# One store for 1/z, keys loaded ahead of queries, and new weights of a list scheduler in an attention and gated-convolution kernel

## The chip, the cores and the metric

The kernel runs on one core of a Trainium2 chip. The metric is the device time of one execution in microseconds (us); lower is better. TensorE is called PE below, VectorE DVE, ScalarE ACT, GpSimd POOL, and SyncE, which issues every DMA of this kernel, SP.

## The reference

```python
def _attn_ref(q, kv, w_sr):            # q: 4 x 12288 x 128, kv: 4 x 384 x 32 x 128
    kv_pool = kv.reshape(B, H // r, r, W // r, r, C).mean(axis=(2, 4))   # r = 4
    kv_flat = kv_pool.reshape(B, -1, C) @ w_sr                           # 768 keys of 128
    k = v = kv_flat
    s = scale * (q @ k.transpose(0, 2, 1))
    s = s - s.max(-1, keepdims=True)
    a = np.exp(s)
    a /= a.sum(-1, keepdims=True) + 1e-09
    return a @ v

def _moe_ref(x, w_val, conv_w, w_out):  # x is the attention's result
    ...
    for k in range(K):                  # 5 taps along the sequence
        gate_pre += conv_w[k][None, None, :] * xp[:, k:k + S, :]
    gate = 1.0 / (1.0 + np.exp(-gate_pre))
    val = x @ w_val
    return (gate * val @ w_out).astype(np.float32)
```

## The kernel before

**Tiling.** There are 4 batches, each with 12288 queries and 768 keys of 128 numbers. A group is 512 queries of one batch, 24 groups to a batch, 96 in all, numbered 0 to 95. Within a group a score tile `s` holds 128 queries (on partitions) by 768 keys; there are four, j = 0 to 3. The host hands over q and kv with the 128 channels on partitions; the kernel writes its result with channels on partitions too.

**A batch's set-up** (`setup`): kv comes in 16 pieces (`kvt`, line 257, six buffers), DVE sums each piece over its 16 pooled positions (L266), PE projects the sums with w_sr (L287), and ACT and DVE split the keys into two parts `kh`, `kl` and the values into `vh`, `vl`. From the second batch on the loads and sums are spread over the groups of the batch before it, about one piece to a group.

**A group** (`group`): q is loaded for two groups at once (L419); ACT and POOL split it into `qh`, `ql`. Per score tile PE does six matmuls (L445), DVE takes the row maximum (L457), ACT the exponential with its row sum z (L471). For j = 0 to 2 ACT and DVE then split the exponentials into two f16 parts `hl` (L487, L498) and SP has them transposed by DMA into `pt` (L510, one DMA for j = 0 and 1, one for j = 2). For j = 3 PE transposes the f32 exponentials in six blocks (L532), and ACT and DVE write the split straight into `pt` (L545, L549). Then 18 matmuls (L610) sum values times `pt` into one PSUM bank `av`.

**1/z** has to lie along the free axis of all partitions to multiply `av`, whose partitions are channels. POOL adds 1e-9 (L569), DVE takes the reciprocal of a 128 x 4 tile (L573) and transposes it in 32 x 32 blocks (L577). Row j of each 32-row block then holds 32 queries of tile j. Four DMAs of 4 rows each write these to a DRAM scratch `rd` (L583), and one DMA reads it back broadcast to all partitions, `rb` (L589). DVE multiplies, x = av * down * rb (L628).

**After x**: POOL makes four of the five taps (L677) and adds them up (L686), ACT makes one tap (L666) and the tanh (L701); PE does x @ w_val (L705), DVE the product (L709), PE the output matmul (L714), ACT the move out of PSUM (L719), and SP stores two groups at once (L739).

**What is single.** There is one `av` bank, so the first L610 matmul of a group has to wait until L628 of the group before has read `av`; one `m` bank for L705 and L714; and three `s` tiles, which the score tiles and the PE transposes share.

**What sets the order.** Every instruction is a step with an engine, an estimated duration, a due time and what it waits for, takes and frees. `Plan.order` is a list scheduler in the program itself: again and again it places, on the engine that can begin first, the step with the least due time among those that could start by then, in times that it estimates. Each engine then carries out its steps strictly in that order. Due times are multiples of `PERIOD` (a group's planned length) and `AV_DUE` written into each step. For SP it reckons 0.06 us per DMA issue, and a DMA queue that takes the steps' durations one after the other:

```python
            if e == "SP":
                free[e] = t + 0.06
                dma = max(dma, t + self.DMA_LEAD) + s.dur
                s.end = dma + self.DMA_TAIL
```

## Time and profile before

| | |
|---|---|
| median of 3 runs | 1136.8 us (1133.98 to 1137.78) |
| the profiled execution's own time | 1133.29 us |
| its span, first to last instruction | 1131.5 us |
| busy share of PE, DVE, ACT, POOL | 93%, 81%, 77%, 78% |
| the 16 DMA engines: share of SP's queue | 86.4% |
| the same execution's granted PE clock, mean | 0.992 of full speed |

The busy shares count an instruction from its start to its end; matmuls overlap one another, so PE's share says that it is seldom without work, not that it is at its peak. The span is cut into four parts further below: the load of the first keys up to about 31 us, a ramp up to the first x at 62.7 us, 95 steps from x to x up to 1116.3 us, and 15 us in which the last group's end runs out.

### The profile page before, as it was taken

The page shows a single profiled execution, that of the slowest core. Times are in us where ns is not written, and L with a number is a line of the kernel's source. Part 1 is how long each engine was busy: PE and PEld are TensorE (multiplying, and loading weights), DVE is VectorE, ACT ScalarE, POOL GpSimd, SP SyncE. Part 2 cuts the span into 40 slices and gives each one's busy share as a digit, 9 for nine tenths or more (in the row PEclk, how much of TensorE's full clock was granted, in tenths as well). Part 3 has the DMA queues.
Part 4 walks back from the last instruction along what each step waited for, and adds up shares of the span by engine and source line. Part 5 has one row for each costly group of instructions (what it writes and reads, how often), then busy time and mean ns, then how long its engine had stood idle before and what let it go on. Part 6 is the DMA issues. An engine that isn't in the chain of part 4 may idle for free.

```text
span 1131.5 us, 16498 instructions
## 1 busy us (share of the span) xinstructions
PE 1050.6 (93%) x5056; PEld 667.7 (59%) x5056; DVE 918.4 (81%) x1280; ACT 869.8 (77%) x1559; POOL 884.2 (78%) x1049
## 2 busy tenths in 40 slices
PE   0799999999999999999999899999999999999996
PEld 0565656666656656666666555665666666666662
DVE  6788887878888988878888888887887788787784
ACT  1577877888777878878888777888888888887872
POOL 1167887888978788888878778888888888888872
PEclk9899999999999999999999999999999999999997
DMA  9488999888899999898999899978888898987774
GB/s 336 101 189 181 224 213 201 164 185 197 200 214 205 230 211 208 186 178 175 215 237 199 188 194 209 202 165 180 190 172 178 188 189 167 178 205 154 154 158 98
DMA packets 488968, 215.54 MB, mean 190 GB/s; under 512 B 455728, under 2 KB 455856, under 8 KB 488880
## 3 DMA queue, kind: packets, MB, share of 16 engines
q1 hardware_dynamic: 488880, 214.49, 86.4%
q8 instruction: 41, 0.67, 0.2%
q14 instruction: 47, 0.39, 0.1%
HBM read 75.83 MB, written 25.36 MB: 89 GB/s over the span
## 4 chain that ended last, share of the span: by engine, by line
PE 68%; DVE 11%; DMA 9%; SPq 4%; issue 3%; ACT 3%; POOL 1%; DVEq 0%
PE s L445 26%; PE av L610 24%; PE m L705 6%; PE m L714 6%; PE s L532 5%; DMA kvt<-in_kv 4%; DMA rb<-rd 3%; DVE nm L457 3%; SPq L510 2%; DVE hl L498 2%; DVE x L628 2%; DVE pool L266 1%; DVE pt L549 1%; SPq L583 1%; ACT s L471 1%
## 5 line engine op out<-in xcount | busy, mean ns | idle before, releaser
L686 POOL TENSOR_TENSOR gate<-gate,tap 128x512 f32<-128x512 f32 x376 | 481.6, 1281 | 14.2
L457 DVE TENSOR_REDUCE nm<-s 128x1 f32<-128x768 f32 x384 | 363.9, 951 | 79.9 <-PE s L445 77.8
L610 PE MATMUL av<-pt,vh 128*128 128x512 f16 x1152 | 374.6, 381 | 19.1 <-DVE x L628 11.9
L471 ACT ACTIVATE s<-s,nm 128x768 f32<-128x768 f32 x288 | 251.8, 874 | 111.8 <-DVE nm L457 110.6
L498 DVE SCALAR_TENSOR_TENSOR hl<-s,hl 128x768 f16<-128x768 f32 x288 | 271.8, 945 | 13.4 <-ACT hl L487 12.4
L445 PE MATMUL s<-kh,qh 128*128 128x512 f32 (+1 forms) x768 | 258.8, 418 | 19.3 <-DVE hl L498 9.6
L487 ACT ACTIVATE hl<-s 128x768 f16<-128x768 f32 x288 | 232.9, 811 | 3.8
L610 PE MATMUL av<-pt,vl 128*128 128x512 f16 x576 | 218.8, 380 | 0.0
L610 PEld LDWEIGHTS <-vh 128*128 128x128 f16 x1152 | 109.6, 98 | 179.0 <-issue 77.0
L445 PE MATMUL s<-kl,qh 128*128 128x512 f32 (+1 forms) x768 | 198.9, 340 | 0.0
L445 PE MATMUL s<-kh,ql 128*128 128x512 f32 (+1 forms) x768 | 197.6, 338 | 0.0
L677 POOL TENSOR_SCALAR tap<-x,wm 128x512 f32<-128x512 f32 x282 | 191.4, 697 | 0.1
L445 PEld LDWEIGHTS s<-kh,qh 128*128 128x128 f32 x768 | 136.9, 191 | 90.9 <-issue 21.0
L677 POOL TENSOR_SCALAR gate<-x,wm 128x512 f32<-128x512 f32 x94 | 65.4, 696 | 137.7 <-DVE x L628 137.6
L431 POOL TENSOR_TENSOR ql<-q,qh 128x512 fp32r<-128x512 f32 x96 | 122.4, 1275 | 59.8 <-ACT qh L427 59.4
L445 PEld LDWEIGHTS s<-kl,qh 128*128 128x128 f32 x768 | 118.8, 190 | 17.4 <-DVE kl L321 0.5
L445 PEld LDWEIGHTS s<-kh,ql 128*128 128x128 f32 x768 | 118.7, 190 | 17.0
L719 ACT ACTIVATE o<-m 128x512 f32<-128x512 f32 x96 | 57.4, 598 | 67.7 <-PE m L714 67.4
L549 DVE SCALAR_TENSOR_TENSOR pt<-s,pt 128x768 f16<-128x768 f32 x96 | 90.9, 947 | 20.1 <-ACT pt L545 19.8
L714 PE MATMUL m<-h,wm 128*128 128x512 f32 x192 | 100.7, 607 | 3.0 <-DVE h L709 2.0
L705 PE MATMUL m<-x,wm 128*128 128x512 f32 x192 | 99.3, 599 | 3.4 <-DVE x L628 2.7
L532 PE MATMUL s<-ident,p 128*128 128x128 f32 x576 | 96.1, 273 | 1.0 <-ACT p L471 1.0
(59 smaller groups left out, 961.2 us busy)
## 6 DMA issues: line engine op xcount, KB each, us to landing
kvt<-in_kv SPq DMA_DIRECT2D x64, 384.0 KB
q<-in_q SPq DMA_DIRECT2D x48, 512.0 KB
rb<-rd SPq DMA_DIRECT2D x96, 256.0 KB
out<-o SPq DMA_DIRECT2D x47, 512.0 KB
rd<-rt SPq DMA_DIRECT2D x384, 0.5 KB
pt<-hl SPq DMA_TRANSPOSE x192
out<-o SPq DMA_DIRECT2D x2, 256.0 KB
raw<-in_w_moe SPq DMA_DIRECT2D x1, 261.0 KB
```

The source lines that it names most:

```text
L431: nc.gpsimd.tensor_tensor(out=g.ql, in0=g.qt[:, i], in1=g.qh.bitcast(F32), op=ALU.subtract)
L445: nc.tensor.matmul(t[:, c0:c1], a[:, sl], k[:, c0:c1], start=(n == 0), stop=(n == 2))
L457: v.tensor_reduce(out=s.tile, in_=sc.tile[:, :NK], axis=AX.X, op=ALU.max, negate=True)
L471: nc.scalar.activation(out=out, in_=sc.tile[:, :NK], func=AF.Exp, bias=mx.tile, accum_out=g.z[:, j:j + 1])
L487: nc.scalar.activation(out=g.hls[j // 2][:, half, 0], in_=sc.tile[:, :NK], func=AF.Copy, scale=2.0 ** 15)
L498: v.scalar_tensor_tensor(out=hl[:, half, 1], in0=sc.tile[:, :NK], scalar=2.0 ** 15, in1=hl[:, half, 0], op0=ALU.mult, op1=ALU.subtract)
L532: nc.tensor.transpose(state["t"][:, k * P:(k + 1) * P], ex.tile[:, k * P:(k + 1) * P], ident)
L610: nc.tensor.matmul(g.av, st[name][:, k * P:(k + 1) * P], g.pt[:, :, a * NCH + k], start=(n == 0), stop=(n == len(AV) - 1))
L677: nc.gpsimd.tensor_scalar(out=s.tile, in0=src(k), scalar1=w[k], scalar2=1.0, op0=ALU.mult, op1=ALU.mult)
L686: nc.gpsimd.tensor_tensor(out=g.gate, in0=g.gate, in1=tap.tile, op=ALU.add)
L705: nc.tensor.matmul(g.m, wval, g.x[:, HALO:], start=True, stop=True)
L714: nc.tensor.matmul(g.m2, wout, g.h, start=True, stop=True)
```

## The change

- **1/z by one store.** The reciprocal is written to columns 0, 8, 16 and 24 of the 32-wide tile, so that after the block transposition the 16 rows wanted lie at partitions 0, 8, 16, ... 120, and one DMA of 16 rows by 32 writes them. The scratch is then in the order (block of 32 rows, tile j, query). So that this is the output's order too, the host permutes the queries within each 512, and the 18 value matmuls read `pt` in that order: 16 runs of 32 elements instead of 4 runs of 128.
- **Keys first.** The first three loads of q may start in the planner's time only at 9, 24 and 28 us (`FIRST_Q`), the load of the gate's weights (`raw`) at 17 us.
- **Copies drawn together.** Of two DMA steps that could start, a copy that follows a copy gets 3.6 us off its due time (`CLUMP`); before, a step that followed one of its kind got 0.3 us on top. The six PE transposes lose their kind, and with it the rule that kept them apart.
- **New weights.** Due times come from one table `DUE`, `PERIOD` is 10.25 for 10.4, durations and lags of the estimates change, an SP issue is reckoned at 0.5 us for a copy and 0.9 of its duration for a transpose.

```diff
-PERIOD = 10.4
+PERIOD = 10.25
+DUE = dict(q=-42.1, qh=-11.9, ql=-12.5, score=-2.2, max=0.8, exp=1.8, hi=4.2, lo=5.4, turn=5.0,
...
-                s = min((s.due + (s.kind != "" and s.kind == last[e]) * 0.3, n, s)
+                s = min((s.due - (s.kind == last[e] == "copy") * self.CLUMP, n, s)
...
             if e == "SP":
-                free[e] = t + 0.06
-                dma = max(dma, t + self.DMA_LEAD) + s.dur
+                copy = s.kind == "copy"
+                free[e] = t + (0.5 if copy else 0.9 * s.dur)
+                switch = 0.6 if last[e] == "copy" and not copy else 0.0
+                dma = max(dma + switch, t + self.DMA_LEAD) + s.dur
                 s.end = dma + self.DMA_TAIL
...
-        s = plan.add("SP", 1.0, 2, lambda: nc.sync.dma_start(out=raw, in_=w_moe.bitcast(I32)))
+        s = plan.add("SP", 1.0, 2, start=17.0, run=lambda: nc.sync.dma_start(out=raw, in_=w_moe.bitcast(I32)))
...
-            ld = plan.add("SP", 1.3, t0 - 4 * T, load, takes=("q",), start=t0 - 5 * T)
+            ld = plan.add("SP", 1.3, t0 + D["q"], load, takes=("q",),
+                          start=FIRST_Q[g.i // 2] if g.i < 6 else t0 + D["q"] - T)
...
-            s = plan.add("ACT", 1.02, t0 + j * T / 4 + 2.2, run, [sc, mx],
+            s = plan.add("ACT", 0.88, t0 + j * T / 4 + D["exp"], run, [sc, mx],
...
-            v.reciprocal(out=g.r[:, :NT], in_=g.ze)
+            v.reciprocal(out=g.r[:, ::32 // NT], in_=g.ze)
...
-        def rd(j):
-            def run():
-                if j == 0:
-                    g.rd = tile_of(s_rd[0], "rd")
-                nc.sync.dma_start(out=g.rd[j].rearrange("(b i) -> b i", i=32),
-                                  in_=g.rt[j::32, :])
-            return run
+        def rd():
+            g.rd = tile_of(s_rd, "rd")
+            nc.sync.dma_start(out=g.rd.rearrange("(a i) -> a i", i=32), in_=g.rt[::32 // NT, :])
...
-                nc.tensor.matmul(g.av, st[name][:, k * P:(k + 1) * P], g.pt[:, :, a * NCH + k],
+                nc.tensor.matmul(g.av, st[name][:, k * P:(k + 1) * P],
+                                 g.pt[:, :, a * NCH + k].rearrange("k j (b i) -> k b j i", i=32),
...
+FIRST_Q = (9.0, 24.0, 28.0)
...
-        "in_q": np.ascontiguousarray(q.transpose(0, 2, 1)),
+        "in_q": np.ascontiguousarray(
+            q.reshape(B, N // GQ, P // 32, NT, 32, C).transpose(0, 5, 1, 3, 2, 4)
+            .reshape(B, C, N)),
```

The new table moves instructions on every engine. Three places follow, all around group 70; a number behind a name tells one allocation of a tile from another. In the lines of the changed kernel L456 is the score matmul, L543 the PE transpose, L614 the value matmul, L633 x, L468 the row maximum, L509 the split, L521 the transposing DMA, L591 and L595 the two DMAs of 1/z.

PE before, from the last value matmul of group 70 (`av_9325`) to the first of group 71 (`av_9449`):

```order
L610 MATMUL av_9325<-pt_9178,vh_5246 128x512
L445 MATMUL s_9430<-kh_6868,qh_9187 128x512
L445 MATMUL s_9430<-kh_6868,qh_9187 128x256
L445 MATMUL s_9430<-kl_6872,qh_9187 128x512
L445 MATMUL s_9430<-kl_6872,qh_9187 128x256
L445 MATMUL s_9430<-kh_6868,ql_9191 128x512
L445 MATMUL s_9430<-kh_6868,ql_9191 128x256
L610 LDWEIGHTS vh_5246
L610 MATMUL av_9449<-pt_9299,vh_5246 128x512
```

PE now, at the same border (`av_9160` to `av_9283`):

```order
L614 MATMUL av_9160<-pt_8940,vh_5431 128x512
L456 MATMUL s_9256<-kh_6935,qh_8960 128x512
L456 MATMUL s_9256<-kh_6935,qh_8960 128x256
L456 MATMUL s_9256<-kl_6980,qh_8960 128x512
L456 MATMUL s_9256<-kl_6980,qh_8960 128x256
L456 MATMUL s_9256<-kh_6935,ql_8974 128x512
L456 MATMUL s_9256<-kh_6935,ql_8974 128x256
L543 MATMUL s_9271<-ident,p_9205 128x128 x6
L614 LDWEIGHTS vh_5431
L614 MATMUL av_9283<-pt_9054,vh_5431 128x512
```

Between the two groups' value matmuls one score tile stood before; now a score tile and the six transposes of another tile stand there.

DVE before, around x of group 70:

```order
L457 TENSOR_REDUCE nm_9387<-s_9357 128x1
L549 SCALAR_TENSOR_TENSOR pt_9299<-s_9336,pt_9299 128x768
L457 TENSOR_REDUCE nm_9409<-s_9395 128x1
L498 SCALAR_TENSOR_TENSOR hl_9367<-s_9357,hl_9367 128x768
L457 TENSOR_REDUCE nm_9426<-s_9415 128x1
L628 SCALAR_TENSOR_TENSOR x_9377<-av_9325,down_5157,rb_9384 128x512
L498 SCALAR_TENSOR_TENSOR hl_9439<-s_9395,hl_9439 128x768
```

DVE now, around the same x:

```order
L468 TENSOR_REDUCE nm_9223<-s_9209 128x1
L587 STREAM_TRANSPOSE rt_9229<-r_63 128x32
L468 TENSOR_REDUCE nm_9248<-s_9231 128x1
L509 SCALAR_TENSOR_TENSOR hl_9246<-s_9209,hl_9246 128x768
L633 SCALAR_TENSOR_TENSOR x_9201<-av_9160,down_5223,rb_9094 128x512
L468 TENSOR_REDUCE nm_9275<-s_9256 128x1
L509 SCALAR_TENSOR_TENSOR hl_9246<-s_9231,hl_9246 128x768
```

x stood right behind a row maximum; now a row maximum and a split stand ahead of it, and the maximum of the score tile at the border comes behind it.

SP before, two groups (`rd_9262` and `rd_9372` are the scratch rows of groups 70 and 71):

```order
L510 DMA_TRANSPOSE pt_9178<-hl_9189 128x12x128
L583 DMA rd_9262<-rt_9258 4x32
L739 DMA out<-o_9141 128x1024
L510 DMA_TRANSPOSE pt_9299<-hl_9241 128x24x128
L583 DMA rd_9262<-rt_9258 4x32 x3
L583 DMA rd_9372<-rt_9370 4x32
L510 DMA_TRANSPOSE pt_9299<-hl_9315 128x12x128
L589 DMA rb_9384<-rd_9262 128x512
L583 DMA rd_9372<-rt_9370 4x32 x3
L510 DMA_TRANSPOSE pt_9428<-hl_9367 128x24x128
L589 DMA rb_9444<-rd_9372 128x512
```

SP now, the stretch with the 1/z of groups 70 (`rb_9094`), 71 and 72:

```order
L521 DMA_TRANSPOSE pt_9054<-hl_8996 128x24x128
L595 DMA rb_9094<-rd_9037 128x512
L743 DMA out<-o_8953 128x1024
L591 DMA rd_9121<-rt_9108 16x32
L521 DMA_TRANSPOSE pt_9054<-hl_9068 128x12x128
L595 DMA rb_9143<-rd_9121 128x512
L521 DMA_TRANSPOSE pt_9176<-hl_9125 128x24x128
L591 DMA rd_9242<-rt_9229 16x32
L521 DMA_TRANSPOSE pt_9176<-hl_9191 128x12x128
L595 DMA rb_9264<-rd_9242 128x512
```

Four stores to a group have become one, and nothing else was added to the queue. In the whole program SP issues 837 DMAs before and 549 now; passages from a copy to a transposing DMA number 191 before and 190 now. In both programs a DMA also waits until the one eight places ahead of it in SP's queue has landed, since eight semaphores go round.

## Rows read from the trace of the kernel before

**Rows 1.** The page: span, busy us of each engine (share of span) and instructions.

```profile
span 1131.5 us, 16498 instructions
PE 1050.6 (93%) x5056; PEld 667.7 (59%) x5056; DVE 918.4 (81%) x1280; ACT 869.8 (77%) x1559; POOL 884.2 (78%) x1049
```

**Rows 2.** Line L628 (x) in five stretches: duration min/median/max, first and last start, count.

```profile
L628 DVE SCALAR_TENSOR_TENSOR x<-av,down,rb x24: 742/742/751, 62.7 to 326.4; 128x512 f32<-128x512 f32 x24
L628 DVE SCALAR_TENSOR_TENSOR x<-av,down,rb x24: 741/742/750, 335.1 to 591.5; 128x512 f32<-128x512 f32 x24
L628 DVE SCALAR_TENSOR_TENSOR x<-av,down,rb x24: 741/742/752, 602.1 to 863.2; 128x512 f32<-128x512 f32 x24
L628 DVE SCALAR_TENSOR_TENSOR x<-av,down,rb x21: 741/742/751, 873.8 to 1091.3; 128x512 f32<-128x512 f32 x21
L628 DVE SCALAR_TENSOR_TENSOR x<-av,down,rb x96: 741/742/752, 62.7 to 1116.3; 128x512 f32<-128x512 f32 x96
```

**Rows 3.** Timeline of PE, 854 to 857 us: start us, us, line, operation, count.

```profile
854.33 0.71 PE L532 MATMUL s<-ident,p 128*128 128x128 f32 x5
854.88 1.02 PE L705 MATMUL m<-x,wm 128*128 128x512 f32 x2
855.74 0.38 PE L610 MATMUL av<-pt,vh 128*128 128x512 f16 x1
855.95 0.38 PE L610 MATMUL av<-pt,vl 128*128 128x512 f16 x1
855.98 0.70 PE L445 MATMUL s<-kh,qh 128*128 128x512 f32 x2
...
857.22 0.59 PE L714 MATMUL m<-h,wm 128*128 128x512 f32 x1
```

**Rows 4.** Groups by shape: the set-up's matmuls of batches 1 to 3, busy us and mean ns.

```profile
L373 PE MATMUL m<-diag,vt 128*128 128x128 f32 x36 | 5.0, 274 | 0.0
L287 PE MATMUL m<-pool,wsr 128*128 128x384 f32 x12 | 4.9, 492 | 0.8 <-DVE pool L266 0.8
```

**Rows 5.** Waits of PE, whole span: us in total, times, longest us.

```profile
PE av L610 <- DVE x L628: 11.9, 19, 1.9
PE s L445 <- DVE hl L498: 9.6, 19, 1.7
PE s L445 <- DVE pt L549: 7.1, 8, 3.1
```

**Rows 6.** Timeline of SP, 4 to 8 us.

```profile
4.03 2.72 SPq L419 DMA_DIRECT2D q<-in_q  x3
7.78 0.33 SPq L237 DMA_DIRECT2D raw<-in_w_moe  x1
```

**Rows 7.** The page's DMA issues: tensors, count, KB each.

```profile
kvt<-in_kv SPq DMA_DIRECT2D x64, 384.0 KB
q<-in_q SPq DMA_DIRECT2D x48, 512.0 KB
raw<-in_w_moe SPq DMA_DIRECT2D x1, 261.0 KB
```

**Rows 8.** Windows, the first 20 us: busy us (x) of each engine, PEclk, DMA share, GB/s.

```profile
0.00:20.00 20.00, 0.91 (x2) 0.50 (x2) 10.18 (x13) 3.04 (x4) 4.61 (x13) 1.00 0.91 342
```

**Rows 9.** Timeline of DVE and PE, 17 to 31 us.

```profile
17.03 0.94 DVE L266 TENSOR_REDUCE pool<-kvt 128x48 f32<-128x768 f32 x1
...
27.75 0.95 DVE L266 TENSOR_REDUCE pool<-kvt 128x48 f32<-128x768 f32 x1
...
30.98 1.01 PE L445 MATMUL s<-kh,qh 128*128 128x512 f32 x2 [0.58 <-ACT kh L297]
```

**Rows 10.** Timeline of SP, 884 to 899 us: start us, us of issuing, line, count.

```profile
883.85 3.62 SPq L510 DMA_TRANSPOSE pt<-hl  x1
887.52 2.26 SPq L583 DMA_DIRECT2D rd<-rt  x4
889.88 1.33 SPq L510 DMA_TRANSPOSE pt<-hl  x1
891.38 0.86 SPq L589 DMA_DIRECT2D rb<-rd  x1
892.30 1.55 SPq L583 DMA_DIRECT2D rd<-rt  x3
```

**Rows 11.** Waits of DVE for DMAs, 60 to 866 us: us in total, times, longest.

```profile
DVE pool L266 <- DMA kvt<-in_kv: 19.9, 16, 2.8
DVE x L628 <- DMA rb<-rd: 5.8, 7, 1.4
```

**Rows 12.** Timeline of DVE and PE at a border of two groups, 849 to 853 us.

```profile
851.09 0.96 DVE L457 TENSOR_REDUCE nm<-s 128x1 f32<-128x768 f32 x1
852.11 0.75 DVE L628 SCALAR_TENSOR_TENSOR x<-av,down,rb 128x512 f32<-128x512 f32 x1
852.77 0.95 DVE L498 SCALAR_TENSOR_TENSOR hl<-s,hl 128x768 f16<-128x768 f32 x1
...
850.90 0.39 PE L610 MATMUL av<-pt,vh 128*128 128x512 f16 x1
...
852.91 0.39 PE L610 MATMUL av<-pt,vh 128*128 128x512 f16 x1 [0.49 <-DVE x L628]
```

**Rows 13.** Timeline of DVE, the last two x.

```profile
1110.01 0.75 DVE L628 SCALAR_TENSOR_TENSOR x<-av,down,rb 128x512 f32<-128x512 f32 x1 [1.68 <-DMA rb<-rd]
1116.26 0.75 DVE L628 SCALAR_TENSOR_TENSOR x<-av,down,rb 128x512 f32<-128x512 f32 x1 [0.37 <-DMA rb<-rd]
```

More of the change, by code (lines that the diff above doesn't have):

```diff
@@ L33 @@
 class Plan:
-    EDGE = 0.08
-    DMA_LEAD, DMA_TAIL = 1.3, 0.8
+    EDGE = 0.04
+    LAG = dict(PE=0.16, ACT=0.1, DVE=0.085, POOL=0.04, SP=0.0)
+    DMA_LEAD, DMA_TAIL, CLUMP = 1.3, 0.8, 3.6
     def __init__(self):
@@ L44, in pool, with add @@
         self.stock[name] = [(0.0, i) for i in range(n)]
-    def add(self, eng, dur, due, run, after=(), takes=(), frees=(), lag=0.1, start=0.0, kind=""):
+    def add(self, eng, dur, due, run, after=(), takes=(), frees=(), lag=None, start=0.0, kind=""):
+        lag = self.LAG[eng] if lag is None else lag
+        if eng == "SP" and not kind:
+            kind = "copy"
         s = Step(eng, dur, due, run, [a for a in after if a], takes, frees, lag, start, kind)
@@ L289, in project @@
                              [load_sr, pools_done[(h + 1) * PIECES // 2 - 1]],
-                             takes=(psum,), frees=[(holder["pool"], "pool")], lag=0.2)
+                             takes=(psum,), frees=[(holder["pool"], "pool")])
                 return s
@@ L432, in ql @@
                                     op=ALU.subtract)
-        s_qh = plan.add("ACT", 0.51, t0 - 1.5 * T, qh, [g.ld], takes=("qh",))
-        s_ql = plan.add("POOL", 1.25, t0 - 1.2 * T, ql, [s_qh], takes=("ql",),
+        s_qh = plan.add("ACT", 0.51, t0 + D["qh"], qh, [g.ld], takes=("qh",))
+        s_ql = plan.add("POOL", 1.25, t0 + D["ql"], ql, [s_qh], takes=("ql",),
                         frees=[(g.ld, "q")])
@@ L449, in score @@
                 frees += [(st["kh_by"], "kh"), (st["kl_by"], "kl")]
-            s = plan.add("PE", 1.065, t0 + j * T / 4, run, [s_qh, s_ql] + st["keys"],
-                         takes=("s",), frees=frees, lag=0.2)
+            s = plan.add("PE", 1.05, t0 + j * T / 4 + D["score"], run, [s_qh, s_ql] + st["keys"],
+                         takes=("s",), frees=frees)
             return s
@@ L458, in run @@
                                 negate=True)
-            s = plan.add("DVE", 0.87, t0 + j * T / 4 + 1.2, run, [sc], takes=("nm",))
+            s = plan.add("DVE", 0.87, t0 + j * T / 4 + D["max"], run, [sc], takes=("nm",))
             return s
@@ L499, in lo @@
                                        in1=hl[:, half, 0], op0=ALU.mult, op1=ALU.subtract)
-            s_lo = plan.add("DVE", 0.865, t0 + j * T / 4 + 4.1, lo, [s_hi], frees=[(sc, "s")])
+            s_lo = plan.add("DVE", 0.865, t0 + j * T / 4 + D["lo"], lo, [s_hi], frees=[(sc, "s")])
             g.los[j] = s_lo
@@ L533, in run @@
                                         ex.tile[:, k * P:(k + 1) * P], ident)
-                s = plan.add("PE", 0.118, t0 + j * T / 4 + 3.6, run, [ex, state.get("by")],
-                             takes=("s",) if k == 0 else (), frees=[(ex, "p")], lag=0.2,
-                             kind="turn")
+                s = plan.add("PE", 0.109, t0 + j * T / 4 + D["pe"], run, [ex, state.get("by")],
+                             takes=("s",) if k == 0 else (), frees=[(ex, "p")])
                 if k == 0:
@@ L550, in lo @@
                                        in1=flat(0), op0=ALU.mult, op1=ALU.subtract)
-            s_hi = plan.add("ACT", 0.71, t0 + j * T / 4 + 4.6, hi, blocks + [g.pt_by])
-            s_lo = plan.add("DVE", 0.865, t0 + j * T / 4 + 5.4, lo, [s_hi],
+            s_hi = plan.add("ACT", 0.71, t0 + j * T / 4 + D["thi"], hi, blocks + [g.pt_by])
+            s_lo = plan.add("DVE", 0.865, t0 + j * T / 4 + D["tlo"], lo, [s_hi],
                             frees=[(blocks[0], "s")])
@@ L631, in group @@
         cont = prev is not None and prev.b == g.b
-        s_halo = plan.add("POOL", 0.15, t0 + (AV_DUE + 0.6) * T, halo,
+        s_halo = plan.add("POOL", 0.15, t0 + D["halo"], halo,
                           [prev.s_x] if cont else [], takes=("x",),
@@ L636, in group @@
         g.s_halo = s_halo
[L637 removed]
+        g.s_x = plan.add("DVE", 0.66, t0 + D["x"], x, [avs[-1], s_rb, s_halo,
                                                                    st["down_by"]],
@@ L666, in run @@
                     nc.scalar.activation(out=s.tile, in_=src(k), func=AF.Copy, scale=w[k])
-                s = plan.add("ACT", 0.61, late - 0.1 * T + (4 - k) * 0.3 * T, run,
+                s = plan.add("ACT", 0.61, t0 + D["tap"], run,
                              [g.s_x, weights_done], takes=(f"tap{k}",), frees=[(s_halo, "x")])
@@ L686, in run @@
                     nc.gpsimd.tensor_tensor(out=g.gate, in0=g.gate, in1=tap.tile, op=ALU.add)
-                return plan.add("POOL", 1.25, late, run, [tap, before],
+                return plan.add("POOL", 1.3, late, run, [tap, before],
                                 frees=[(tap, f"tap{k}")])
```

66 lines of the change are left out of this document (31 added, 35 removed).

## The prediction, made before the changed kernel was run

> **What bounds the kernel now.** I read the page's busy times first: PE has work for 93% of the span, DVE for 81%, ACT and POOL for less [rows 1]. So the question is what PE's pace is, and what it would be without waits. The starts of x, one to a group, give the pace: from 62.7 to 1116.3 us in 95 steps, 11.09 us a step. By batch it is 11.47, 11.15 and 11.35 us for the three that load the next batch's keys meanwhile (23 steps each), and 10.88 us for the last, which loads none (20 steps) [rows 2].
>
> PE's own work in a group is read from starts in its timeline, since the durations of matmuls overlap: five transposes take 854.33 to 854.88, 0.11 us each; L705 to the next start 0.86; one value matmul 0.21; a score tile 1.06, which is 1.27 from the value matmul at 855.95 to 857.22, less that matmul [rows 3]. Six transposes, L705 and L714, 18 value matmuls and four score tiles make 0.66 + 1.72 + 3.78 + 4.24 = 10.4 us. The last batch thus loses 0.5 us a group, the other three 0.9 (11.32 on average). Set-up accounts for a little of that: its 48 matmuls are busy for 9.9 us in all, 0.14 us a group of those batches [rows 4]. All losses together, 20 x 0.5 + 72 x 0.9, are about 75 us, and 65 without set-up. That is what an order can win back; the rest is PE's work, the head and the end.
>
> The list of PE's waits tells which ones are met most: x, which holds the one `av` bank (11.9 us in 19 waits), and the two splits L498 and L549, which free `s` tiles (9.6 and 7.1 us) [rows 5]. These are only the waits in which PE stood quite idle, so they are lower bounds.
>
> **The change, part by part.**
>
> *Keys first.* Three loads of q and `raw` are issued ahead of the seventh key piece [rows 6], and a fourth q ahead of the thirteenth: 16 x 384 + 64 (w_sr) + 4 x 512 + 261 = 8517 KB up to the last piece. Now two q loads are ahead: 7232 KB, 7.4 MB [rows 7]. At the 342 GB/s of the first 20 us [rows 8] that is 21.7 us. Before, the last key sum begins at 27.75, in a row of sums from 17.03 on between which the weights' arithmetic stands; the first score begins 3.2 us after it [rows 9]. If DVE begins its last sum at 22 to 23, the first score comes 5 us sooner. The weights' arithmetic isn't saved, though: what DVE did while it waited for keys now falls among the first groups' maxima. I charge 1 us for it. Net -4; the bounds are -6 (all of 27.75 less 21.7) and 0 (the ramp takes as much longer).
>
> *One store.* Four stores take SP 2.26 us to issue, 0.565 each. A group's two transposes (3.62 and 1.33), its `rb` (0.86) and its stores thus hold the queue for 8.1 of some 11 us before any load or output; from 883.85 to 893.85, where stores of two groups meet, it is 9.6 of 10.0 [rows 10]. Three issues, 1.7 us, leave the queue in each group. Nobody waits for SP itself; those that wait for its DMAs are DVE's key sums (19.9 us in 16 waits) and x (5.8 us in 7), in the stretch with key loads [rows 11]. DVE's steps behind them, maxima and splits, are what PE's `s` tiles wait for. The loading batches lose 0.44 us a group more than the last one, 32 us in 72 groups, or 22 us without set-up, which agrees with DVE's 25.7 us. A wait for keys is 1.2 us on average, less than the 1.7 us that each load gains in the queue. For x, the change in order does it: `rb` of group 70 stood a transpose and more behind its stores and now is issued ahead of group 71's second transpose, about a group earlier. I take 18 of the 22 us. Bounds: 0, if the loads are late for want of DMA bandwidth and not of issuing, and -22.
>
> The Trainium skill (DMA: Bandwidth & Descriptors, section "Issuing engines are not separate DMA queues") calls the time to initiate a DMA usually small beside the DMA itself; by that rule this term is near 0 and the sum 1115. The trace disagrees as far as issuing goes, with 8.1 us of it in a group.
>
> *The order around x.* At the border shown, the last value matmul starts at 850.90, x starts at 852.11, right as the maximum ahead of it ends, and the next value matmul at 852.91 [rows 12]. So 1.80 us are needed behind the last matmul's own 0.21, and one score tile covers 1.06. Over the 95 borders of the built programs, 17 had a score tile alone, 2 less than that, 31 a score tile and L705 (1.92). Now 45 have a score tile and six transposes (1.72), 7 a score tile or less, and 43 at least 1.47, mostly 1.9 and more. In the new order x follows a maximum and a split whose score tile ends five value matmuls (1.05) before the group's last. The maximum begins some 0.2 after the tile, it and the split take about 0.9 each until the next can start, x to the next matmul 0.80 [rows 12]: 0.2 + 1.8 + 0.8 - 1.05 = 1.75, against a cover of 1.72. This just closes; 45 borders lose 0.03 to 0.1, 7 lose 0.7. Against 11.9 us I take a gain of 6; bounds 0 and -11.
>
> *New weights.* With an exponential reckoned at 0.88 for 1.02 and SP's issues reckoned at all, the order is made for times like those of the trace. Whether `s` tiles come free sooner can't be counted in an order. The waits for splits are 16.7 us [rows 5]; I take -6, about a third. Bounds: -12, and a loss for which see the third rival.
>
> *The end.* The last two x waited 1.68 and 0.37 us for `rb` [rows 13]: three of the four stores stood between the last transpose and `rb`; now none does. I take -2; bounds -2 and 0.
>
> *The reading order of `pt`.* The value matmuls read 16 runs of 32 instead of 4 runs of 128. Before, breaks between runs show no price: a value matmul takes 0.21 us for 512 columns in 4 runs, a score tile's pair of matmuls 1.06/3 = 0.35 for 768 columns in whole rows, 0.24 for 512 [rows 3]. I take 0. The other end is the fourth rival.
>
> The sum: -4 - 18 - 6 - 6 - 2 = -36 us on the profiled execution's own 1133.3 us (span 1131.5 [rows 1] and 1.8 around it), which gives 1097. The median of the runs is 3.5 us above that execution; the range takes this in.
>
> **The rivals.**
>
> *Issuing was not it.* The loads come late because 16 DMA engines are full, and an emptier SP changes nothing: the 18 us fall away, 1115 us. For it: the DMA engines' share is 0.91 at the start [rows 8], and key loads add to the transposes' traffic. Against it: what is waited for are the DMAs that stand behind other issues, and SP issues for most of a group.
>
> *More than counted.* The regular new order runs at its planned fit: 0.15 us lost a group besides set-up. Then 65 us of losses become 14, and with head and end it is -57: 1076. For it: PE's order in the steady part of the last batches is the same from group to group. Against it: each border closes with hundredths to spare.
>
> *Tiles too tight (the slow side).* In the new order the six transposes need the `s` tile that the split ahead of x frees. By the terms above that split ends 0.2 + 0.9 + 0.95 = 2.05 us after its neighbour's score tile; PE gets there after five value matmuls and a score tile, 1.05 + 1.06 = 2.11. The next score tile waits for the next split in the same way. If ACT or DVE is late by half a microsecond at both, PE loses up to 1 us a group. All gains together are 36/96 = 0.38 us a group: from there on the change is a loss. At 0.5 us a group, 1133 - 36 + 48 = 1145. For it: the waits met before at such places lasted 0.5 and 0.9 us on average [rows 5]. Against it: a PE that is late finds the tile free, so that waits do not add up.
>
> *Short runs slow the value matmuls (slow side too).* 1728 value matmuls; 21 ns more on each, a tenth of 0.21 us, cancel the 36 us: 1133. Nothing in the trace speaks for it but that no such read is in it. The Trainium skill (Advanced Engine Details and Errata, "SBUF Cachelines") has full performance where accesses hit a 16-byte line at least twice; by it runs of 64 bytes cost nothing, and no row here shows it.
>
> **How the numbers follow.** Forecast, 1085 to 1110: 0.52. Issuing was not it, 1110 to 1122: 0.16. More than counted, 1070 to 1085: 0.14. Tiles too tight: 0.12, two thirds of it slower, one third no change. Short runs: 0.06, half slower, half no change. A difference of 0.3% (3.4 us) is about what this kernel's measurement can tell from none. Faster by more: 0.52 + 0.16 + 0.14 = 0.82; slower 0.08 + 0.03 = 0.11; same 0.07. Leaving out the slow cases, 0.18, the range is 1072 to 1122.
>
> **What would show it.** The first score at about 26 us; x to x near 10.9 in the loading batches (11.32 less 18/72 and 12/95) and 10.75 in the last; one store of some 0.55 us to a group; DVE's waits for key pieces under 8 us in all and those for `rb` gone; PE's waits for x under 6 us. The forecast is wrong if value matmuls start more than 0.23 us apart, if waits of PE for the splits grow beyond 30 us, or if the three loading batches still run at 11.2.

## The result and the profile after

The changed kernel takes 1088.3 us (median of 4 runs, 1084.95 to 1089.09) against 1135.4 for the kernel before beside it (4 runs, 1132.05 to 1137.78): a ratio of 0.958, 95% interval 0.955 to 0.962. The forecast was 1097, range 1072 to 1122: the direction and the range held, and the gain was 47 us where 36 had been worked out.

The page of the changed kernel, span and busy time, against [rows 1]:

```profile
span 1087.3 us, 16058 instructions
PE 1041.3 (96%) x5056; PEld 664.4 (61%) x5056; DVE 916.6 (84%) x1280; ACT 873.1 (80%) x1559; POOL 876.7 (81%) x1049
```

The starts of x (now L633), cut at the batches as in [rows 2]:

```profile
L633 DVE SCALAR_TENSOR_TENSOR x<-av,down,rb x24: 720/742/752, 58.8 to 311.2; 128x512 f32<-128x512 f32 x24
L633 DVE SCALAR_TENSOR_TENSOR x<-av,down,rb x24: 741/742/743, 321.9 to 574.4; 128x512 f32<-128x512 f32 x24
L633 DVE SCALAR_TENSOR_TENSOR x<-av,down,rb x24: 741/742/744, 585.1 to 831.5; 128x512 f32<-128x512 f32 x24
L633 DVE SCALAR_TENSOR_TENSOR x<-av,down,rb x20: 742/742/742, 842.1 to 1043.5; 128x512 f32<-128x512 f32 x20
L633 DVE SCALAR_TENSOR_TENSOR x<-av,down,rb x96: 720/742/752, 58.8 to 1074.8; 128x512 f32<-128x512 f32 x96
```

The steps are 10.97, 10.98 and 10.71 us in the three loading batches (mean 10.89, before 11.32) and 10.60 in the last (before 10.87). On the profiled spans the first x comes 3.9 us sooner, the 95 steps take 1016.1 us for 1053.6, and from the last x to the end it is 12.4 us for 15.3: 3.9 + 37.5 + 2.8 = 44.2, the whole difference of the two spans.

PE's waits over the whole span behind that for the first keys, against [rows 5]. L543 is the transpose, L559 and L509 the two splits on DVE:

```profile
PE s L543 <- DVE hl L509: 8.9, 3, 4.0
...
PE av L614 <- DVE x L633: 2.0, 3, 0.9
...
PE s L456 <- DVE pt L559: 1.0, 1, 1.0
PE s L456 <- DVE hl L509: 0.8, 2, 0.4
```

Waits for x fell from 11.9 us to 2.0; those of the score tiles for the splits from 16.7 to 1.8. New is the first line: the transposes now wait for a split's `s` tile, three times, but long.

DVE's waits for DMAs between 55 and 830 us, against [rows 11]. `rb` no longer stands in the list; the key pieces do:

```profile
DVE pool L276 <- DMA kvt<-in_kv: 11.1, 7, 3.1
```

Both belong together. In the timelines of DVE (two pieces) and PE at 285 us, a key sum stands 2.45 us for its load. The maxima behind it are late, and with them ACT's exponential and first half of the split; so DVE's split waits 0.73 us for ACT, and PE's transposes stand 1.84 us for that split:

```profile
285.29 0.95 DVE L276 TENSOR_REDUCE pool<-kvt 128x48 f32<-128x768 f32 x1 [2.45 <-DMA kvt<-in_kv]
...
289.01 0.96 DVE L509 SCALAR_TENSOR_TENSOR hl<-s,hl 128x768 f16<-128x768 f32 x1 [0.73 <-ACT hl L498]
...
290.11 0.30 PE L543 MATMUL s<-ident,p 128*128 128x128 f32 x1 [1.84 <-DVE hl L509]
```

A long wait of PE can cost more than itself. The next one, at 550 us, lasts 3.15 us. In it the granted clock of PE falls to 0.50 of full speed (1.2 of 2.4 GHz) and stays there for 6.8 us; six transposes then take 1.51 us, where they take 0.84 at the border shown below. The transposes, and the clock in a window (third number from the end):

```profile
550.53 1.51 PE L543 MATMUL s<-ident,p 128*128 128x128 f32 x6 [3.15 <-DVE hl L509]
...
549.80:556.60 6.80, 6.07 (x17) 3.86 (x18) 4.71 (x7) 4.81 (x9) 5.29 (x7) 0.50 0.76 173
```

The border of two groups now, PE and then DVE, against [rows 12]:

```profile
883.49 0.38 PE L614 MATMUL av<-pt,vh 128*128 128x512 f16 x1
883.52 0.70 PE L456 MATMUL s<-kh,qh 128*128 128x512 f32 x2
...
884.78 0.84 PE L543 MATMUL s<-ident,p 128*128 128x128 f32 x6
885.46 0.38 PE L614 MATMUL av<-pt,vh 128*128 128x512 f16 x1
...
883.69 0.95 DVE L509 SCALAR_TENSOR_TENSOR hl<-s,hl 128x768 f16<-128x768 f32 x1
884.55 0.74 DVE L633 SCALAR_TENSOR_TENSOR x<-av,down,rb 128x512 f32<-128x512 f32 x1
```

From value matmul to value matmul it is 1.97 us, for 0.21 + 1.06 + 0.66 = 1.93 of PE's work. x starts 1.06 behind the last value matmul, as the split ahead of it lets it, and the next value matmul follows x by 0.91.

SP's timeline, against [rows 10]: one store of 0.49 us between two transposes, and stretches in which SP issues nothing (875.06 to 876.48, 880.26 to 881.77). The traces count 835 DMAs of SP before and 547 now, two fewer each than said further above, with the same difference of 288.

```profile
874.73 0.33 SPq L595 DMA_DIRECT2D rb<-rd  x1
876.48 3.78 SPq L521 DMA_TRANSPOSE pt<-hl  x1
881.77 0.49 SPq L591 DMA_DIRECT2D rd<-rt  x1
882.35 1.30 SPq L521 DMA_TRANSPOSE pt<-hl  x1
```

The head (last key sum on DVE, first score on PE) and DVE's last two x, against [rows 9] and [rows 13]. The last x wait for value matmuls now or for nothing, not for `rb`:

```profile
25.60 0.95 DVE L276 TENSOR_REDUCE pool<-kvt 128x48 f32<-128x768 f32 x1 [0.88 <-PE s L297]
...
26.14 1.01 PE L456 MATMUL s<-kh,qh 128*128 128x512 f32 x2 [0.58 <-ACT kh L307]
...
1068.54 0.75 DVE L633 SCALAR_TENSOR_TENSOR x<-av,down,rb 128x512 f32<-128x512 f32 x1 [1.87 <-PE av L614]
1074.84 0.74 DVE L633 SCALAR_TENSOR_TENSOR x<-av,down,rb 128x512 f32<-128x512 f32 x1
```

The end behind the last x differs by something else: PE's granted clock. In the profiled execution of the kernel before it fell to 0.50 at 1120.0, after PE had stood idle for 2.68 us before 1110.91 and for 1.18 us before 1118.25, and stayed there to the end. In the changed kernel it stayed at full speed over this work. A pair of output matmuls before, the clock there (third number from the end), and such a pair now:

```profile
1120.06 2.07 PE L714 MATMUL m<-h,wm 128*128 128x512 f32 x2 [0.69 <-ACT o L719]
1120.00:1131.50 11.50, 6.22 (x6) 1.50 (x6) 1.87 (x3) 1.72 (x4) 0.00 (x0) 0.50 0.23 91
...
1082.49 1.12 PE L719 MATMUL m<-h,wm 128*128 128x512 f32 x2 [0.86 <-DVE h L714]
```

Three such pairs, each 0.95 us longer, make up the 2.8 us.

### The profile page after: what moved, and what is told of

It is laid out like the page before. It is cut to its first block, busy times and chain, and to the rows that moved or that the text cites. A ratio compares the mean times of both kernels' runs of the same rounds, so it can differ in the third digit from the quotient of the medians.

```text
span 1087.3 us, 16058 instructions
## 1 busy us (share of the span) xinstructions
PE 1041.3 (96%) x5056; PEld 664.4 (61%) x5056; DVE 916.6 (84%) x1280; ACT 873.1 (80%) x1559; POOL 876.7 (81%) x1049
## 3 DMA queue, kind: packets, MB, share of 16 engines
q1 hardware_dynamic: 488880, 214.49, 91.3%
## 4 chain that ended last, share of the span: by engine, by line
PE 88%; DMA 5%; DVE 4%; ACT 1%; issue 1%; POOL 1%; SPq 1%; DVEq 0%
PE s L456 35%; PE av L614 32%; PE m L719 7%; PE m L710 7%; PE s L543 6%; DMA kvt<-in_kv 4%; DVE nm L468 1%; DVE hl L509 1%; DMA pt<-hl 1%; ACT hl L498 0%; DVE pool L276 0%; DMA rd<-rt 0%; PE m L383 0%; PE m L297 0%; POOL gate L691 0%
## 5 line engine op out<-in xcount | busy, mean ns | idle before, releaser
L468 DVE TENSOR_REDUCE nm<-s 128x1 f32<-128x768 f32 x384 | 364.2, 950 | 92.5 <-PE s L456 90.5
L614 PE MATMUL av<-pt,vh 128*128 128x512 f16 x1152 | 375.6, 381 | 2.0 <-DVE x L633 2.0
L509 DVE SCALAR_TENSOR_TENSOR hl<-s,hl 128x768 f16<-128x768 f32 x288 | 272.4, 946 | 5.5 <-ACT hl L498 5.3
L456 PE MATMUL s<-kh,qh 128*128 128x512 f32 (+1 forms) x768 | 266.9, 428 | 2.8 <-DVE pt L559 1.0
L614 PE MATMUL av<-pt,vl 128*128 128x512 f16 x576 | 220.0, 382 | 0.0
L456 PEld LDWEIGHTS s<-kh,qh 128*128 128x128 f32 x768 | 140.0, 192 | 97.2 <-PE av L614 27.4
L456 PE MATMUL s<-kl,qh 128*128 128x512 f32 (+1 forms) x768 | 198.3, 339 | 0.0
L456 PE MATMUL s<-kh,ql 128*128 128x512 f32 (+1 forms) x768 | 197.2, 338 | 0.0
L614 PEld LDWEIGHTS <-vh 128*128 128x128 f16 x1152 | 107.0, 98 | 121.4 <-issue 48.8
L456 PEld LDWEIGHTS s<-kl,qh 128*128 128x128 f32 x768 | 118.5, 190 | 17.5 <-DVE kl L331 0.5
L456 PEld LDWEIGHTS s<-kh,ql 128*128 128x128 f32 x768 | 118.4, 189 | 16.7
L482 ACT ACTIVATE p<-s,nm 128x768 f32<-128x768 f32 x96 | 87.0, 906 | 35.9 <-DVE nm L468 34.9
L559 DVE SCALAR_TENSOR_TENSOR pt<-s,pt 128x768 f16<-128x768 f32 x96 | 91.3, 952 | 11.6 <-ACT pt L555 11.2
L614 PEld LDWEIGHTS <-vl 128*128 128x128 f16 x576 | 56.3, 98 | 72.5 <-issue 43.7
```

Source lines behind the costliest of these rows:

```text
L456: nc.tensor.matmul(t[:, c0:c1], a[:, sl], k[:, c0:c1], start=(n == 0), stop=(n == 2))
L468: v.tensor_reduce(out=s.tile, in_=sc.tile[:, :NK], axis=AX.X, op=ALU.max, negate=True)
L482: nc.scalar.activation(out=out, in_=sc.tile[:, :NK], func=AF.Exp, bias=mx.tile, accum_out=g.z[:, j:j + 1])
L509: v.scalar_tensor_tensor(out=hl[:, half, 1], in0=sc.tile[:, :NK], scalar=2.0 ** 15, in1=hl[:, half, 0], op0=ALU.mult, op1=ALU.subtract)
L559: v.scalar_tensor_tensor(out=flat(1), in0=state["t"][:, :NK], scalar=2.0 ** 15, in1=flat(0), op0=ALU.mult, op1=ALU.subtract)
L614: nc.tensor.matmul(g.av, st[name][:, k * P:(k + 1) * P], g.pt[:, :, a * NCH + k].rearrange("k j (b i) -> k b j i", i=32), start=(n == 0), ...
```

## The experiments

Theory A is the forecast's: SP's issuing makes key loads and 1/z late, and the order of the table does the rest. The rivals stand in each expectation. Ratios are to the kernel before (1134.7 to 1135.4 us beside each run), with 95% intervals. The steps are from x to x, "load" the mean of the three loading batches; "DMA waits" are DVE's for key pieces and for 1/z over the whole span.

| kernel | us | ratio | load | last | DMA waits |
|---|---|---|---|---|---|
| before | 1135.4 | 1 | 11.32 | 10.87 | 25.8 + 8.3 |
| changed | 1088.3 | 0.958 (0.955 to 0.962) | 10.89 | 10.60 | 18.3 + 0 |
| before, one store | 1121.5 | 0.989 (0.987 to 0.992) | 11.14 | 10.86 | 19.2 + 0 |
| before, keys first | 1137.3 | 1.001 (0.998 to 1.004) | 11.32 | 10.89 | 30.1 + 6.7 |
| changed, four stores planned | 1110.6 | 0.979 (0.976 to 0.982) | 11.18 | 10.61 | 39.8 + 2.4 |
| changed, order kept, four stores | 1116.3 | 0.984 (0.982 to 0.986) | 11.27 | 10.60 | 43.2 + 0 |
| changed, long runs | 1087.9 | 0.959 (0.955 to 0.962) | 10.86 | 10.60 | 18.2 + 0 |
| changed, SP reckoned at 0.06 | 1089.9 | 0.960 (0.956 to 0.965) | 10.90 | 10.60 | 22.0 + 0 |
| changed, old load order | 1086.4 | 0.958 (0.954 to 0.961) | 10.76 | 10.60 | 15.9 + 0 |
| changed, x due later | 1087.4 | 0.959 (0.955 to 0.963) | 10.88 | 10.60 | 18.2 + 0 |
| changed, transposes due early | 1120.4 | 0.987 (0.986 to 0.989) | 11.29 | 10.95 | 24.6 + 0 |
| changed, key sums late | 1076.9 | 0.949 (0.947 to 0.950) | 10.76 | 10.60 | 9.4 + 0 |
| the same, old load order | 1080.9 | 0.953 (0.951 to 0.954) | 10.69 | 10.60 | 9.7 + 0 |
| key sums late, four stores | 1105.6 | 0.976 (0.971 to 0.981) | 11.16 | 10.61 | 33.2 + 0 |

**Four stores in the changed order.**

```diff
-            nc.sync.dma_start(out=g.rd.rearrange("(a i) -> a i", i=32), in_=g.rt[::32 // NT, :])
+            rows16 = g.rd.rearrange("(a i) -> a i", i=32)
+            for b in range(NT):
+                nc.sync.dma_start(out=rows16[b * NT:(b + 1) * NT],
+                                  in_=g.rt[b * 32:(b + 1) * 32:32 // NT, :])
```

> The changed kernel with its order on every engine kept, but each group's 1/z goes out by four stores of 4 rows, issued one behind the other where the one store stood: 288 DMAs more on SP's queue. Theory A, that SP's issuing is what the loads and transposes wait for: three issues of about 0.55 us a group take back what the store was counted at, 10 to 18 us, and DVE's waits for key pieces and for 1/z grow by as much. Rival B, that the order of the instructions made the gain and not SP's time: at most 3 us slower.

28 us slower with the same bytes and the same order: A holds, and the price was set too low. SP's timeline of this kernel, and then DVE's waits in it (55 to 830 us):

```profile
105.16 0.42 SPq L267 DMA_DIRECT2D kvt<-in_kv  x1
105.64 2.39 SPq L593 DMA_DIRECT2D rd<-rt  x4
108.08 2.02 SPq L521 DMA_TRANSPOSE pt<-hl  x1
```

```profile
DVE pool L276 <- DMA kvt<-in_kv: 35.9, 19, 6.0
```

Four stores hold SP 2.39 us where one takes 0.49, and DVE's waits for keys go from 11.1 to 35.9 us. The last batch, which loads no keys, stays at 10.60. The Trainium skill (DMA: Bandwidth & Descriptors, "Issuing engines are not separate DMA queues") calls the time to start a DMA usually small beside the DMA itself. For one DMA that is so here: a store of the changed kernel holds SP 0.49 us and lands 3.0 us (median) after its issue. What does not follow is that the term is near 0, as the prediction had it by that rule: the sum of 288 such times cost 28 us.

The 16 DMA engines were not what filled up: SP's queue kept them busy for 85.8% of the span here, 91.3% in the changed kernel. Part of the 28 us may be PE's clock: behind the first x it stood at 0.50 for 20.4 us (from 100.2, 192.4, 557.6 and 642.9 us on), in the changed kernel for 6.8. Each of these stretches began in a wait of PE of 2.5 to 5.4 us or 1 us behind one. At half speed the difference is at most 6.8 us, an estimate.

**Four stores, planned.** The one step of the list scheduler becomes four; the order is made anew.

```diff
-        s_rd = plan.add("SP", 0.03, t0 + D["rd"], rd, [s_rt], takes=("rd",),
-                        frees=[(s_rt, "rt")])
+        s_rd = []
+        for b in range(NT):
+            s_rd.append(plan.add("SP", 0.03, t0 + D["rd"], rd(b), [s_rt] + s_rd[:1], ...
```

> The changed kernel with four stores as four steps of the list scheduler, which makes its order anew with them; table, durations, keys first and reading order as in the changed kernel. Theory A (SP's issuing): 1100 to 1110 us, 12 to 20 slower than the changed kernel. Rival B (the table and the order around x made most of the gain): within 4 us of the changed kernel.

22 us slower than the changed kernel (A had 12 to 20), all of it in the batches that load keys; with everything but the store the change is still 24 us faster than before.

**One store in the kernel before.** The host's order and the reading order of the value matmuls come with it, as in the change.

```diff
-            v.reciprocal(out=g.r[:, :NT], in_=g.ze)
+            v.reciprocal(out=g.r[:, ::32 // NT], in_=g.ze)
...
-        s_rd = []
-        for j in range(NT):
-            s_rd.append(plan.add("SP", 0.03, t0 + 1.2 * T, rd(j), [s_rt] + s_rd[:1], ...
+        s_rd = plan.add("SP", 0.03, t0 + 1.2 * T, rd, [s_rt], takes=("rd",),
```

> The kernel before with one store for 1/z, the host's order and the reading order of the value matmuls that go with it; the old due times, durations and load order stay. Theory A: 15 to 20 us faster than before, about 1117, with DVE's waits for keys in the loading batches down from 19.9 to under 8 us and those for 1/z gone. Rival B: at most 5 us faster. If the 16 short runs cost a value matmul anything, this run is slower than before.

13 us faster, less than A's 15 to 20 and more than B's 5. The waits for 1/z are gone, as A has it, but those for keys only fell to 19.2 us. DVE's waits for DMAs fell by 14.9 us together. In the profiled spans the 95 steps take 9.6 us less (1044.0), and the end is 2.8 shorter, as the clock falls only 2.4 us before it is over:

```profile
DVE pool L266 <- DMA kvt<-in_kv: 19.2, 16, 4.1
```

**Keys first, alone in each kernel.** In the kernel before:

```diff
-        s = plan.add("SP", 1.0, 2, lambda: nc.sync.dma_start(out=raw, in_=w_moe.bitcast(I32)))
+        s = plan.add("SP", 1.0, 2, start=17.0, run=lambda: nc.sync.dma_start(out=raw, in_=w_moe.bitcast(I32)))
...
-            ld = plan.add("SP", 1.3, t0 - 4 * T, load, takes=("q",), start=t0 - 5 * T)
+            ld = plan.add("SP", 1.3, t0 - 4 * T, load, takes=("q",),
+                          start=FIRST_Q[g.i // 2] if g.i < 6 else t0 - 5 * T)
```

> The kernel before with the first three loads of q and the load of the gate's weights held back in the planner's time, nothing else. Forecast: first score about 26 us instead of 30.98, and 4 us faster in all. Rival: the ramp behind it takes as much longer, and the time is that of the kernel before within 1 us; or, as all later steps are placed anew, a few us either way that come from the order further on.

The first score came at 26.32 us and the first x 4.2 us sooner, and the 95 steps took 5.8 us longer (1059.4). The end was 2.9 us shorter, again with the clock up for most of it. The medians of the two kernels do not differ. The reverse, the old load order in the changed kernel:

```diff
-        s = plan.add("SP", 1.0, 2, start=17.0, run=lambda: nc.sync.dma_start(out=raw, in_=w_moe.bitcast(I32)))
+        s = plan.add("SP", 1.0, 2, run=lambda: nc.sync.dma_start(out=raw, in_=w_moe.bitcast(I32)))
...
-                          start=FIRST_Q[g.i // 2] if g.i < 6 else t0 + D["q"] - T)
+                          start=t0 + D["q"] - T)
```

> The changed kernel with the first q loads and the gate's weights loaded ahead of the keys again. Forecast's step: first score back at about 31 us and 4 us slower in all. Rival, from the run in which keys first alone won nothing in the kernel before: the order made anew decides more than the head, and the time is within 3 us of the changed kernel or over 8 us above it, with the difference behind x of group 0.

The first x came 6.6 us later and the 95 steps took 8.6 us less (1007.4). Both times the head moved the way that was forecast, and the order made anew with it moved the steps behind it the other way.

**Long runs.** The value matmuls read 4 runs of 128 again.

```diff
-                                 g.pt[:, :, a * NCH + k].rearrange("k j (b i) -> k b j i", i=32),
+                                 g.pt[:, :, a * NCH + k],
```

> The changed kernel, same order on every engine, but the 18 value matmuls of a group read their 512 columns as 4 runs of 128 again. Its result therefore multiplies each query by the 1/z of another one; the work is the same. Forecast's step (the reading order costs nothing): within 2 us of the changed kernel, value matmuls 0.2155 us apart in both. Rival (short runs cost 1 to 5 ns a matmul that other gains hid): 2 to 9 us faster.

0.4 us from the changed kernel. The groups by shape, of the changed kernel and of this run, differ in no digit that matters:

```profile
L614 PE MATMUL av<-pt,vh 128*128 128x512 f16 x1152 | 375.6, 381 | 2.0 <-DVE x L633 2.0
```

```profile
L614 PE MATMUL av<-pt,vh 128*128 128x512 f16 x1152 | 375.6, 381 | 1.9 <-DVE x L633 1.9
```

**The planner's view of SP, and x due later.** Two edits of the planner:

```diff
-                free[e] = t + (0.5 if copy else 0.9 * s.dur)
-                switch = 0.6 if last[e] == "copy" and not copy else 0.0
+                free[e] = t + 0.06
+                switch = 0.0 if last[e] == "copy" and not copy else 0.0
```

> The changed kernel with the list scheduler's old view of SP: an issue takes it 0.06 us, and no switch between copies and transposes; the table, the durations and the one store stay. All orders are made anew. Theory A' (the order fits because SP's issuing is reckoned, so that sums and x are placed when their DMA has really landed): 8 to 15 us slower than the changed kernel, with DVE's waits for keys and 1/z up. Rival B' (due times and durations of PE, ACT and DVE make the fit): within 4 us, and the last batch still at 10.6 us a group.

```diff
-           avs=9.4, halo=26.6, x=33.1, ...
+           avs=9.4, halo=26.6, x=34.4, ...
```

> The changed kernel with x due 1.3 us later, 9.9 us behind the first value matmul as in the kernel before (8.6 in the new table); all else as changed. Theory A'' (the place of x among maxima and splits made the value matmuls' wait go): PE's waits for x grow from 2.0 us to 8 or more, the last batch goes from 10.6 to about 10.7 us a group, and the whole is 4 to 10 us slower. Rival: x finds its place all the same, within 3 us.

Neither moves the time (1.6 and 0.9 us apart from the changed kernel, intervals overlapping). With CLUMP at 0 the list scheduler makes the very same program: "copies drawn together" does nothing here.

**Transposes due early.**

```diff
-           pe=5.7, thi=2.0, tlo=1.0, ...
+           pe=3.6, thi=2.0, tlo=1.0, ...
```

> The changed kernel with one number of the table changed back: the six PE transposes are due 3.6 us into their slot and not 5.7. In the order made anew 69 of the 95 borders between two groups' value matmuls then have a score tile alone (5 in the changed kernel), and none the six transposes. Theory C (as the forecast had it: x needs 1.75 us and more behind the last value matmul, so a score tile of 1.06 leaves 0.6 to 0.9 us open): 40 to 55 us slower, the last batch at 11.2 us a group. Rival D (what counts is when x itself starts: 0.42 us behind the last value matmul's start if DVE is free then, and 0.85 later the next value matmul runs, which one score tile just covers): the last batch stays within 0.1 of 10.6, and the whole within 10 us of the changed kernel, unless the s tiles are then late.

32 us slower, less than C and far more than D; D had named the exception, `s` tiles that are late, and that is what the rows show. PE and then DVE at a border of the last batch, and below two of PE's waits (55 to 1105 us):

```profile
952.49 0.38 PE L614 MATMUL av<-pt,vh 128*128 128x512 f16 x1
953.13 0.59 PE L456 MATMUL s<-kh,qh 128*128 128x512 f32 x2 [0.26 <-DVE hl L509]
...
954.26 0.39 PE L614 MATMUL av<-pt,vh 128*128 128x512 f16 x1
...
952.03 0.95 DVE L509 SCALAR_TENSOR_TENSOR hl<-s,hl 128x768 f16<-128x768 f32 x1
952.91 0.75 DVE L633 SCALAR_TENSOR_TENSOR x<-av,down,rb 128x512 f32<-128x512 f32 x1
```

```profile
PE s L456 <- DVE hl L509: 22.2, 53, 3.3
PE av L614 <- DVE x L633: 5.6, 4, 3.7
```

x starts 0.42 us behind the last value matmul, as D had it, and PE hardly waits for x. It waits for the `s` tile instead: the score tile starts 0.64 behind the value matmul, when the split has freed its bank. The border takes 1.77 us for 1.27 of work.

**Key sums late.** The scheduler takes the key loads of batches 1 to 3 to land 3 us later.

```diff
-                s.end = dma + self.DMA_TAIL
+                s.end = dma + self.DMA_TAIL + s.lag
...
-                         takes=("kvt",), start=at(i))
+                         takes=("kvt",), start=at(i), lag=0.0 if first else 3.0)
```

> The changed kernel, but the list scheduler takes the key loads of batches 1 to 3 to land 3 us later than it did, so that DVE's key sums are placed later behind the same loads; the whole order is made anew. Theory A: DVE's waits for keys (11.1 us in 55 to 830) fall below 4, PE's waits for the splits ahead of its transposes (8.9 us) with them, and the kernel is 5 to 8 us faster, about 1081. Rival: the waits were short enough to lie beside other work, or come back at other places of an order made anew: within 3 us.

11 us faster than the changed kernel, more than A's 5 to 8, and the best of all. PE's clock, too, does not fall to half again behind the first x (6.8 us of it in the changed kernel). DVE's waits for keys (55 to 830 us) and PE's transposes (whole span):

```profile
DVE pool L276 <- DMA kvt<-in_kv: 1.1, 1, 1.1
...
PE s L543 <- DVE hl L509: 2.5, 2, 2.3
```

It also has 15 borders with a score tile alone, and each shows the border without loss. PE, then DVE:

```profile
380.24 0.38 PE L614 MATMUL av<-pt,vh 128*128 128x512 f16 x1
380.27 0.70 PE L456 MATMUL s<-kh,qh 128*128 128x512 f32 x2
...
381.51 0.39 PE L614 MATMUL av<-pt,vh 128*128 128x512 f16 x1
...
380.66 0.75 DVE L633 SCALAR_TENSOR_TENSOR x<-av,down,rb 128x512 f32<-128x512 f32 x1
```

1.27 us for 1.27 of work: x starts 0.42 behind the value matmul, and the next one follows x by 0.85.

The same edit together with the old load order, as in the diff further above:

> The same as the run with the key sums late, and also the first q loads and the gate's weights ahead of the keys as in the kernel before. From the run with those loads alone (0.2 us a group gained in the first two loading batches, 6.5 us lost ahead of the first x): if the late sums already take away the waits that it saved, it is 4 to 6 us slower than the run with the key sums late alone; if the first groups' loads matter by themselves, within 2 us.

4.0 us slower than with the key sums late alone, the size that the forecast gave the head. The spans show that it is a difference of two: the first x comes 9.0 us later (66.7 for 57.7), and the 95 steps take 3.4 less (1002.4 for 1005.8).

**Key sums late, four stores.** The first experiment's diff on top of the late key sums.

> The run with the key sums late, its order kept, but with four stores of 4 rows in the place of the one, as in the run with the changed kernel's order kept (which was 28 us slower, with DVE's waits for keys in 55 to 830 us up from 11.1 to 35.9). Theory A: the stores cost through those waits alone, and sums placed 3 us later absorb most of the lateness: waits for keys under 15 us and 5 to 12 us slower than with one store. Rival E: SP's queue is full in the loading batches, its lateness adds up from group to group, and no fixed slack holds it: waits for keys over 25 us, or as much again for the transposes, and 20 to 30 us slower.

E: 29 us slower than with one store, and the waits for keys (55 to 830 us) are back, fewer than in the changed order's four stores but longer:

```profile
DVE pool L276 <- DMA kvt<-in_kv: 26.2, 13, 6.8
```

## Why the prediction was right, point by point

On the spans the 44.2 us divide by the run with four planned stores: its first x comes 4.0 us sooner than before, its 95 steps take 15.8 us less, its end 2.7 less, and the one store takes another 21.7 off the steps. The starts of x in that run:

```profile
L640 DVE SCALAR_TENSOR_TENSOR x<-av,down,rb x96: 718/741/751, 58.7 to 1096.5; 128x512 f32<-128x512 f32 x96
```

This division hangs on which part comes first. With the one store put into the kernel before, it takes 9.6 us off the steps, and the rest of the change 27.9. Some 12 us of the gain thus need both the store and the new order, and neither part's worth is one number.

- **One store, -18 forecast.** -22 in the new order, -13 in the old one, +28 if taken back with the order kept. The mechanism is shown: nothing but DMAs of the same bytes in all was added, the price fell on the loading batches, and DVE's waits grew by 24.8 us, against 28 in the time. The bound of -22 came from the loading batches' excess over the last one in the old order (0.31 us a group without set-up). That excess is no bound once the order is faster: in the new one four stores leave 11.18 against 10.61. "Issuing was not it" has fallen. Whether the price is SP's time as such or the places that DMAs take in the ring of eight semaphores, no run separates. SP's own list of waits speaks against the ring: in the run with the order kept it has 2.6 us for DMAs other than the stores that `rb` reads and the last outputs.
- **Waits for keys under 8 us:** missed, 11.1. "Less than the 1.7 us that each load gains in the queue" took a load to gain on average what a wait costs on average; seven waits of up to 3.1 us stayed. The scheduler places the sums where it believes the loads to have landed; with that belief 3 us later, 1.1 us was left and the kernel gained 11 us.
- **Order around x and new weights, -12 together:** -15.8, or -27.9 with the one store already in. The step that was mis-sized is the measure: half of the waits for x and "about a third" of those for splits. PE's list of waits can't carry such shares. The kernel with four planned stores has 30.4 us of waits for x and splits, those ahead of the transposes among them, more than the 28.6 of [rows 5], and yet its steps are 15.8 us shorter:

```profile
PE av L621 <- DVE x L640: 14.1, 9, 2.8
PE s L543 <- DVE hl L509: 8.1, 5, 3.9
PE s L456 <- DVE pt L559: 5.5, 4, 3.1
PE s L456 <- DVE hl L509: 2.7, 4, 1.1
```

  The last batch shows the gain undisturbed: 10.87 to 10.60, 5.4 us in 20 steps, of which PE stood idle for x in 3.6 us before and in none now. The forecast had 10.75 there. It had left out the last three steps, in which the last groups run out: they give another 4.2 us (24.96 to 20.74).
- **The border.** "1.80 us are needed behind the last matmul's own 0.21" was wrong as a need: x can start 0.42 behind the value matmul's start, and then 1.27 suffice, with a score tile alone. It started 1.21 behind it in [rows 12] because a maximum stood ahead of it. What the 45 borders with six transposes lose (0.04) was forecast rightly; that the cover made the gain was not. (Before, the trace has 35 borders with a score tile and L705, not 31; the sum doesn't use that count.) The run with transposes due early shows the pair: PE waits either for x or for the `s` tile that a split frees, and the order must serve both.
- **Keys first, -4:** the head moved by 3.9, as forecast. As a gain of its own it does not stand: alone in the kernel before it brought nothing, and taken back in the changed kernel nothing was lost. That the term fits the spans is in part luck. With the key waits gone, taking it back cost 4.0 us. The forecast had looked for the giving back in the ramp; it came in the steps behind the first x.
- **The end, -2:** no x waits for `rb` any more, but the -2.8 behind the last x agrees by luck: it is PE's clock, which fell in this one execution of the kernel before. Every other kernel ends in 12.4 to 12.8 us, that with four stores and only the keys first too. The two waits for `rb` lie ahead of the last x, in the last three steps, and taking them away gave nothing there: with one store in the old order these steps take 25.57 us (24.96 before), with four stores in the new order 20.73. What the term had wrong is the path: without waits for `rb` these x come no sooner; under the new table they do, with one store or four.
- **The reading order, 0:** 0.4 us measured. "Short runs" has fallen. That agrees with the Trainium skill (Advanced Engine Details and Errata, "SBUF Cachelines"), which has full performance where accesses hit a 16-byte line at least twice.
- **Tiles too tight:** the place was right, the frequency not. It is 8.9 us in three waits, not one in each group: one of 4.0 us in the ramp, the two later ones behind late key sums, at 285 and 550 us, both shown above.

Open: which of the table's other numbers the 15.8 us hang on. SP's reckoning, the clump and x's due time are none of them; the transposes' due time is one (32 us if undone); durations and lags weren't tried apart.

## What to carry to other kernels

On a queue that one engine issues, count the issues of each group against its period: 288 more stores of 0.5 KB each cost 28 us, and only where somebody waited for a DMA behind them. Where a planner places the consumers of loads, give it the landing times of the trace, a little late rather than early: here a sum that waited for its load held up everything behind it on its engine, while sums placed later cost nothing that the time shows. And size a reordering by the pace of an undisturbed stretch, not by shares of the list of waits, and by a run with that part alone: each order made anew moved these times by several us by itself.

## What the runs showed of the hardware

The time that a transposing DMA holds SP isn't fixed. Summed from SP's rows between 330 and 595 us, 96 stores took 54.5 us and 48 transposes 139.4 before (2.90 each); now 23 stores take 13.8 and 49 transposes 161.6 (3.30 each, up to 6.66). Whether the emptier queue lengthens them is open. One store in the old order goes with 3.19 each in the same stretch, against 2.90 with four; but four stores in the changed order go with 3.20, hardly less than the changed kernel's 3.30.

With four stores in the changed order SP issued for 0.93 of the time from 866 to 1080 us, in the last batch, and the steps there stayed at 10.60: a nearly full issuing engine cost nothing by itself. From 62 to 866 us, where the 28 us were lost, it issued for 0.90.

PE's granted clock fell to 0.50 in, or 1 us behind, waits of PE of 2.5 to 5.4 us in the middle of two of these kernels, and at that level a pair of 512-column f32 matmuls took 2.07 us for 1.12. A wait of PE can thus cost more than its length.
